# Another written order, with other PSUM slots and masks, for a fused threshold-attention and maxout-FFN kernel

## The chip, the cores and the metric

The kernel runs on one core of a Trainium2 chip. The metric is the device time in microseconds (us) of one execution. The runs of the kernel before took 441.89 to 442.23 us, median 441.96 of three.

The engines are named as in the profile: PE is TensorE (matmuls; PEld are its weight loads), DVE is VectorE, ACT is ScalarE, POOL is GpSimd, and SP issues most of the DMAs. Each engine takes its own instructions strictly in the order in which they are written; between engines semaphores hold an instruction back until its inputs are there and its output buffer is free.

## The reference

Attention over 8 batches, 8 heads, 576 tokens and head size 64, in which only scores within tau = 0.02 of the row's maximum count, and then an FFN whose hidden value is the maximum of three projections:

```python
scores = scale * np.matmul(q, k.transpose(0, 1, 3, 2))
thresh = np.max(scores, axis=-1, keepdims=True) - tau
scores = np.where(scores >= thresh, scores, -1000000000.0)
attn = np.exp(scores - np.max(scores, axis=-1, keepdims=True))
attn = attn / (np.sum(attn, axis=-1, keepdims=True) + 1e-09)
x = np.matmul(attn, v).transpose(0, 2, 1, 3).reshape(4608, 512)
h = np.maximum(np.maximum(x @ w1, x @ w2), x @ w3)      # 512 -> 768
return h @ w_out                                         # 768 -> 512
```

## The kernel before

A batch is handled in two quads of four heads. A quad is nine chunks of 128 rows of two heads each, and a chunk is two halves of 128 rows by 576 scores; in all 144 chunks and 288 halves. The work of the whole kernel is cut into small steps, and one string, `ORDER`, says in which order the steps are written. Every letter is one step; a digit behind a capital letter is the PSUM slot (0 to 3, two banks each) into which a step of TensorE writes. All instructions of an engine are held in this written order, so the string sets five queues at once.

The steps, by letter:

- `l` one load of q, k or v by SP (the tiles `qm`, `km`, `q8`/`k8`, printed as `q_..`/`k_..`, `vm`, `vr`); `g` one load of FFN weights by SP into `stage`; `z` its cast by POOL into `w` or `wo`; `y` a cast of v by POOL (`vb`, `vr`).
- `T` transposes q or k of a quad on TensorE into PSUM (tile `tp`), four such steps a quad. `a` copies q out of the slot on ACT (tile `qt`), `c` copies k out of it, mostly on DVE (tile `kt`); `q` copies `qt` with its partition halves swapped into `qs`, mostly on POOL.
- `S` the scores of one half, on TensorE into a slot (tile `sc`). `m` the row's maximum (or negated minimum), DVE, which also writes the half to SBUF as `z`; a few halves of `z` lie in spare `stage` buffers. Then there are two ways. A half with mask 0 or 2 gets `s` on DVE (a 128x1 threshold, `th`; not for mask 2), `e` on ACT (a steep ramp below the threshold), `n` on ACT (Exp with the row's sum). A masked half, 1 or 3, gets `e` on ACT (Exp) and `k` on DVE (zero below the threshold, and the sum). With masks 2 and 3 `e` reads the PSUM slot itself, so the slot is let go by ACT's `e`; with 0 and 1 by DVE's `m`.
- `r` reciprocal of a chunk's sums, DVE. `p` normalizes one half on POOL (tile `P`, bf16), two a chunk. `t` turns a chunk's P by a transposing DMA of SP into `ptq`.
- `O` the product of P and v on TensorE (tile `o`), four a batch, each reading a quad's nine turned chunks; `w` and `x` copy it out on DVE and ACT (tile `xt`, the FFN's input). All four of a batch must be copied before its first FFN piece.
- `F` the first half of an FFN piece, `B` its second half (the row halves of the array are used by two accumulations, which then change places); 18 hidden pieces (`ph`) a batch, copied out by `h` (ACT) and `v` (DVE, a maximum), and two output pieces (`po`), copied out by `u` (ACT) and stored by `o` (SP). `N`, `j`, `i` are the last ninth of the tokens; `f` and `d` the very last output.

The function `issue` takes a letter, takes the next item of that step's queue, and writes its instructions:

```python
        if what == "S":
            c, r = next(todo["S"])
            c[r] = scores(Ls[c["g"]], c["idx"], r, where)
            line["m"].append((c, r))
        ...
        elif what == "t":
            turned(line["t"].pop(0))
```

`_Ordered` adds the dependence that holds each engine's instructions in this order, so nearly all of them carry its line, L93, in the profile; they are told apart by their tiles. `MASKED` has one digit for each half.

Of the kernel before, what the change touches and what calls it, by code (L numbers as in the profile page):

```python
# [21 lines left out]
FLAT = 2.0 ** -100  # L22

MASKED = """
220202110002002100110000100020020312000112012010100000000010100000001100
001000111010000101100000000000110001100000011110110200100000100010000000
110001101110100100010000001001100100000100101111102300000100100000001000
001000110100100001000000000100100001011110100011011100002100001000001013
"""


# [11 lines left out]
meS0kynS2tssT3snkynkercperlT3pmnpmntqremS0lasprgeT3pmeS2psstnplnS0mzecesqrmS3etqkeS2gpnmS1npsmtnS0prmleS3pmS  # L43
2npsmnS0yrsmetperS2epmO1eqtnkplemnzswT2teS3rplS1empnmS3tpnssrS1klepS0mapermtS2epmT1S3nmqtnkO2qemncpS3txrskT1
peS2rmeS0ptmegpamS2npS1ertsmpnlkzS2elmS3eS0mpnlO1srkepsmnO2tyeprgwnpmT1xS3cpeS0sszmF2eS1meBqkF0ngqT3shrsmBay
S2tvpnF3rpemS1BpemF0pnsvT2BnyctS1esrlsT2mphS3lezS1maF0myntpT2sS3ngrcqF1eBmpnS2svpBnrmS3peS0tmeyF2zmnF3lBsvep
S0rhkBptesF2mgeS1zvF0nsmBpteBsrgvpnF1kS3phS2semBnqmF0S3evqF2ntrmBpelS1spvBnlmS3qhF0rsmepS1tnBpsmS3ezvS2eS1rm
pF0etsyO3mnlkngpO2eswetkBxrmpT3nF2rvpaS1BnqmS0hspS3meF2prS1smntBzesmF3ezvT0tBeclT1yS2pnvS0apsmtS3eyrmlS1epS2
mepF0mnqsmnS3tkBnkeF1restpkumeS2prtBumlperkpS0ustS2umS3pesmS1eqtT0mO2nlpceqsrmO3ntywelkS0pxlS1meF3prnS2smBye
myF0thpskS1oeBpF2nlvF3nlrmBpeBkpS1hstsvS0eF3lrmpnF2mBepBsveF1nT0vBtarkS3lhqS2smleF0prF1mnBysntBveS2plvnS0pom  # L50
F3nyS1pmeBsysmF0thT2rrlpeS1clF3epsmBnqT2svBaS1evqS2nmF0pS3nmqBtnmT2pS1hrcpS3esmS0petF2melS1rmpBnF3skpetF0sve
BlBmnF2vhtF1esrBkpnS0vtT3npBmS2arvpS0ermO3eqtsmepT1swntpS0cF2epesmtnS3kT1nS0mtBessrkpameS3preS1mS0uqmuS3mpnS
1tsmS2pnoS0rempS3lempO1lnkqlemO2lnymeO0srkpetkeF3swxykxpT2BercnprtS1uyS2upmF0termqS3eBymN2lhsskpelkS0eF3ertm
S1pjBlmeS0plvF2npS1mnyF3tpmnBsopT0nvBaS1kF2ieqrssmS0hlpBmelT1qF3snrvF0epcBlepS2vBnpsmtS1nS3rmphS2mnpF1smeS0B
snmF3tevS2T0mF1atBrsekpBevS0thS2pmF3nymS1qeBrsmnpS0tvF2eplF1rmnpBskeBptF3hsvS0eBrsstpmnS1lvT2qeO0mpnlscnT3wS
# [774 lines left out]
```

## Time and profile before

| | |
|---|---|
| median of three runs | 441.96 us |
| profiled execution | 442.03 us |
| its span, first to last instruction | 440.2 us |
| busy: PE / DVE / ACT / POOL | 418.9 / 393.9 / 403.6 / 317.0 us |
| mean granted TensorE clock | 0.988 |
| bytes moved by DMA | 88.50 MB |

How to read it: a line of a group has the operation, the tile written and the tiles read, the shapes and the count, then busy time and the mean ns of one. In a listing by time the first number is the start in us from the span's start, the second the length; rows that follow each other are merged, with their count behind an x. A bracket holds the idle time of the engine just before the row, and what ended it. SPq are instructions of SP's queue: their length is the issue, and the data lands later. PE's matmuls are pipelined and their ends modelled.

### The profile page before, as it was taken

The numbers are of one execution on the slowest core, as the hardware profiler recorded it, in microseconds if no ns is written. First come the engines' busy times: TensorE is split into PE (matmuls) and PEld (weight loads), VectorE is DVE, ScalarE is ACT, GpSimd is POOL, SyncE is SP. The second block draws the span as 40 slices with busy tenths as digits, with TensorE's granted clock in tenths as the row PEclk, the third lists the DMA queues.
The fourth block names the chain that finished last, engine by engine and source line by source line (L and its number), as shares of the span: only waits on it lengthen the run. The fifth ranks groups of instructions, "written<-read, shape, count | busy, mean of one in ns | idle before, by whom it ended". The sixth has DMA issues, their size and how long they took to land.

```text
span 440.2 us, 14283 instructions
## 1 busy us (share of the span) xinstructions
PE 418.9 (95%) x5188; PEld 313.6 (71%) x5190; DVE 393.9 (89%) x1248; ACT 403.6 (92%) x834; POOL 317.0 (72%) x420
## 2 busy tenths in 40 slices
PE   7696789999999999999999999999999999999996
PEld 6353446787788776787678777887688777786873
DVE  4888899999999999999999999999889999998542
ACT  4999999999999999999999999999999998989521
POOL 1988999998787778867786778886585776554400
PEclk9987999999999999999999999999999999999999
DMA  6999999999999999999999999999698778583812
GB/s 190 276 239 214 270 215 260 263 252 252 220 277 224 237 165 242 291 160 232 189 242 238 202 182 273 192 199 208 135 237 153 147 109 185 102 169 72 192 50 85
DMA packets 213959, 88.50 MB, mean 201 GB/s; under 512 B 189184, under 2 KB 202240, under 8 KB 213888
## 3 DMA queue, kind: packets, MB, share of 16 engines
q1 hardware_dynamic: 213360, 86.96, 95.4%
q8 instruction: 41, 0.67, 0.6%
q10 hardware_dynamic: 528, 0.62, 0.5%
q14 instruction: 30, 0.25, 0.2%
HBM read 35.65 MB, written 9.44 MB: 102 GB/s over the span
## 4 chain that ended last, share of the span: by engine, by line
PE 78%; DVE 5%; POOL 5%; issue 4%; ACT 3%; DMA 2%; SPq 1%; DVEq 0%; POOLq 0%; ACTq 0%
PE ph L93 31%; PE sc L93 26%; PE po L93 10%; PE o L93 8%; POOL P L93 4%; PE tp L93 3%; ACT z L93 3%; DVE z L93 3%; DMA qm<-in_q_dram 2%; SPq L93 1%; DVE kt L93 1%; POOL w L93 1%; DVE stage L93 0%; DVE hm L93 0%; POOL qs L93 0%
## 5 line engine op out<-in xcount | busy, mean ns | idle before, releaser
L93 POOL TENSOR_SCALAR P<-z,rs 128x576 bf16<-128x576 f32 x250 | 202.0, 819 | 59.1 <-DVE rs L93 30.4
L93 DVE TENSOR_SCALAR_CACHE_REDUCE z<-sc 128x576 f32<-128x576 f32 x250 | 183.2, 749 | 12.2 <-PE sc L93 8.1
L93 PE MATMUL sc<-kt,qs 64*128 64x256 f32 (+2 forms) x640 | 179.8, 417 | 5.5 <-DVE z L93 3.9
L93 PE MATMUL sc<-kt,qt 64*128 64x320 f32 (+2 forms) x640 | 180.9, 429 | 3.1 <-DVE z L93 1.2
L93 PE MATMUL ph<-xt,w 64*128 64x288 bf16 (+2 forms) x2160 | 172.0, 283 | 0.2 <-DVE hm L93 0.2
L93 PEld LDWEIGHTS <-w 64*128 64x128 bf16 (+1 forms) x2160 | 128.0, 94 | 31.6 <-issue 4.0
L93 ACT ACTIVATE z<-z,th 128x576 f32<-128x576 f32 x161 | 120.5, 767 | 2.2 <-DVE th L93 1.9
L93 ACT ACTIVATE z<-z 128x576 f32<-128x576 f32 x175 | 117.6, 674 | 0.2
L93 PEld LDWEIGHTS sc<-kt,qs 64*128 64x128 f32 (+1 forms) x640 | 92.4, 179 | 22.5 <-DVE z L93 8.6
L93 PEld LDWEIGHTS sc<-kt,qt 64*128 64x128 f32 (+1 forms) x640 | 92.0, 179 | 14.7 <-DVE z L93 3.5
L93 DVE SCALAR_TENSOR_TENSOR z<-z 128x576 f32<-128x576 f32 x75 | 61.7, 827 | 1.4 <-ACT z L93 1.1
L93 POOL COPY qs<-qt 64x640 f32<-64x640 f32 (+3 forms) x66 | 45.9, 695 | 19.5 <-ACT qt L93 16.1
L93 ACT ACTIVATE z<-z,nm 128x576 f32<-128x576 f32 x72 | 53.9, 767 | 0.0
L93 PE MATMUL po<-wo,hT 64*128 64x512 bf16 (+3 forms) x454 | 53.3, 354 | 0.3
L93 DVE TENSOR_TENSOR hm<-ph,hm 128x576 bf16<-128x576 f32 (+2 forms) x54 | 37.0, 685 | 9.8 <-PE ph L93 9.6
L93 ACT ACTIVATE hm<-ph 128x576 bf16<-128x576 f32 (+2 forms) x54 | 31.9, 590 | 14.3 <-PE ph L93 13.8
L93 PEld LDWEIGHTS <-hT 64*128 64x128 bf16 (+2 forms) x456 | 28.4, 95 | 18.5 <-issue 2.6
L93 DVE TENSOR_TENSOR hT<-ph,hm 128x576 bf16<-128x576 f32 (+2 forms) x54 | 36.9, 683 | 2.8 <-PE ph L93 1.0
L93 PE MATMUL o<-ptq,vb 128*64 128x512 bf16 (+2 forms) x544 | 38.7, 282 | 0.2 <-DVE z L93 0.2
L93 POOL TENSOR_SCALAR P<-stage,rs 128x576 bf16<-128x576 f32 x38 | 29.5, 783 | 11.7 <-DVE rs L93 8.4
L93 ACT ACTIVATION_READ_ACCUMULATOR z<-z 128x1 f32 x175 | 33.6, 192 | 0.0
L93 PEld LDWEIGHTS <-vb 128*64 128x64 bf16 x544 | 22.4, 111 | 14.0 <-issue 5.6
(44 smaller groups left out, 412.2 us busy)
## 6 DMA issues: line engine op xcount, KB each, us to landing
vm<-in_v_dram SPq DMA_DIRECT2D x32, 256.0 KB, 4.6
qm<-in_q_dram SPq DMA_DIRECT2D x15, 512.0 KB, 4.7
km<-in_k_dram SPq DMA_DIRECT2D x15, 512.0 KB, 5.4
out_dram<-ob SPq DMA_DIRECT2D x14, 512.0 KB, 4.5
stage<-in_moe_w_dram SPq DMA_DIRECT2D x9, 512.0 KB, 5.6
ptq<-P SPq DMA_TRANSPOSE x144, 4.5
vr<-in_v_dram SPq DMA_DIRECT2D x16, 128.0 KB, 3.8
stage<-in_moe_w_out_dram SPq DMA_DIRECT2D x3, 512.0 KB, 5.5
```

Source lines behind the costliest of these rows:

```text
L93: ins = fn(*a, **kw)
```

## The change

The change gives `ORDER` and `MASKED` other values. The steps, the functions and the tiles stay as they are. The string has the same steps in the same numbers but for three letters: `s` 191 in place of 187, `n` 199 in place of 201, `k` 89 in place of 87. Steps stand a few letters earlier or later than before nearly everywhere, and most slot digits are different. Of the 288 digits of the masks, 0 goes from 187 to 191, 1 stays at 84, 2 goes from 14 to 8 and 3 from 3 to 5: masked halves (1 or 3) are 89 in place of 87, halves whose `e` reads PSUM (2 or 3) are 13 in place of 17.

```diff
 MASKED = """
-220202110002002100110000100020020312000112012010100000000010100000001100
+200201101002000000030000103012000330000120210110100001000000100000010110
...
 ORDER = """
-lllllllllT0laqqlcT1aS2lcqqgmS0S3lemS1lmnT2lmeS3lsaS0mnqlqemT3lyerclcapsnS1lS2eqmlS3qemznmS2perS1mnpsmnpT3ske
-ytS1erkpT2agmnT3pclesqS2aqetS0meqlrnspmS1eqsT2nmpS3tnrcS0zlemS2eprmS3npmtS0npsgS1sermpS2emyS3eptmT0eplmS1ayl
...
+lllllllllT1lcaqqlT0S1alcqqmgS3S0elmlnS1smlT3emS2laS0scnqlmT3qelmyS2anlS0mqelqsmezS1lcnrmS3gperpS1nmS0pesmS2y
+ekT3pknT1tressmparmleqcT2lnS3qkeS1pasmetS2prmelpsS3nlmpnsmS2peT1tssqmelycnS2qezmS1nS0rssptnS2rS3gpemynmetrsp
...
```

How it moves instructions, at three places. The first is DVE's queue at the very start: `qs` and `kt` are the copies of the transposed q and k, and the TENSOR_SCALAR rows are the maxima of the first scores. Before:

```order
L93 MEMSET vr_102 64x64 x2
L93 COPY qs<-qt 64x320
L93 COPY kt<-tp 128x320
L93 COPY qs<-qt 64x256
L93 TENSOR_SCALAR z,nm<-sc 128x576 x4
L93 TENSOR_SCALAR th<-nm 128x1
```

and after:

```order
L93 MEMSET vr_102 64x64 x2
L93 COPY kt<-tp 128x320
L93 COPY qs<-qt 64x320
L93 COPY qs<-qt 64x256
L93 TENSOR_SCALAR z,nm<-sc 128x576 x2
L93 TENSOR_SCALAR th<-nm 128x1
```

The first copy of k now stands ahead of the first copy of q, and the first threshold two maxima earlier.

The second is TensorE's queue where quad 1 is transposed for the first time (in the string `T3`, `T2`, `T3` before and `T3`, `T1`, `T2` after; the order does not print the slots). The rows with `qm` and `q_147` are the transposes of q, those with `km` and `k_149` of k, and `sc` are scores. Before:

```order
L93 MATMUL tp<-identf,qm 128x64 x8
L93 MATMUL tp<-identf,q_147 128x64 x2
L93 MATMUL sc<-kt,qs 128x320
L93 MATMUL sc<-kt,qt 128x256
L93 MATMUL tp<-identf,km 128x64 x8
L93 MATMUL tp<-identf,k_149 128x64 x2
L93 MATMUL tp<-identf,qm 128x64 x8
```

and after:

```order
L93 MATMUL sc<-kt,qs 128x320
L93 MATMUL sc<-kt,qt 128x256
L93 MATMUL sc<-kt,qs 128x256
L93 MATMUL sc<-kt,qt 128x320
L93 MATMUL tp<-identf,qm 128x64 x8
L93 MATMUL tp<-identf,q_147 128x64 x2
L93 MATMUL tp<-identf,km 128x64 x8
L93 MATMUL tp<-identf,k_149 128x64 x2
L93 MATMUL tp<-identf,qm 128x64 x8
```

Two scores that stood among or behind the transposes now stand ahead of them, and the three transposes follow each other, in slots 3, 1 and 2.

The third is SP's queue from the ninth transposing DMA (the last of quad 0) to what follows the eighteenth (the last of quad 1). Before:

```order
L93 DMA_TRANSPOSE ptq<-P 128x9x128
L93 DMA stage<-in_moe_w_dram 128x4x256
L93 DMA_TRANSPOSE ptq<-P 128x9x128
L93 DMA km<-in_k_dram 128x2x512
L93 DMA_TRANSPOSE ptq<-P 128x9x128 x2
L93 DMA vm<-in_v_dram 64x4x256
L93 DMA_TRANSPOSE ptq<-P 128x9x128
L93 DMA vm<-in_v_dram 64x4x256
L93 DMA_TRANSPOSE ptq<-P 128x9x128
L93 DMA q_902<-in_q_dram 128x4x64
L93 DMA_TRANSPOSE ptq<-P 128x9x128 x4
L93 DMA stage<-in_moe_w_dram 128x4x256
```

and after:

```order
L93 DMA_TRANSPOSE ptq<-P 128x9x128
L93 DMA km<-in_k_dram 128x2x512
L93 DMA_TRANSPOSE ptq<-P 128x9x128 x5
L93 DMA vm<-in_v_dram 64x4x256
L93 DMA_TRANSPOSE ptq<-P 128x9x128 x4
L93 DMA stage<-in_moe_w_dram 128x4x256
L93 DMA vm<-in_v_dram 64x4x256
L93 DMA q_1040<-in_q_dram 128x4x64
L93 DMA k_1042<-in_k_dram 128x4x64
L93 DMA qm<-in_q_dram 128x2x512
```

Between the ninth and the eighteenth there stand two other DMAs in place of five; one `stage` load has moved ahead of the ninth, and a `vm`, the `q` and others now follow the eighteenth.

More of the change, by code (lines that the diff above doesn't have):

```diff
@@ L24 @@
 MASKED = """
[L25 to L28 removed]
+200201101002000000030000103012000330000120210110100001000000100000010110
+001001100010001010110000000000110000110010111010001000100000100010000100
+100000111101000100010000001001010000000101101101111000101000010000001000
+001001111011000010000000001000100000010101210010010011002000010100101031
 """
@@ L46 @@
[L46 to L55, printed above, removed]
@@ new lines @@
+ptS0resmS2pesmepS3tmepS1rmnpT0tknO3qersmteqkapS2wntS1pslerS3mpnmS2ptnsmS1perT0smS3eptmnpcO1eztrsekS0qemS2xmp
+ntS1mpegS0rmnplS3nmplemlS0qnrsS1klpT2egmO3elpsmaS0knqO2rwetpmeS1pxsrskS3epF2emS0ynmT1pBnmzS3hrcF0eymT2qBgask
+F3peS1sveBtprsmS2ezvnT1F0mpnT3BctapS2hrkqS3ntF0meslrpmT2eS1gzcBnsmS3eptS2vnpF1gmnS0psrsmeS3pseBmqF2esmS0tpeB
+vyF3nmS1hrkBpnF2tveF0pmBntyBsvnqS3lrF1eyrsmpS2hsBptemF0lpesS3vBnzlsmF2nlvS1pnS3rmqBetmF0phgS1npBmeS3yvS2etS1
+srmepF0lknpO3mezsnmO2terkpBgwxF1epvT3S2ktaBrnmlqS0hssS3rpmeF2spS1tsemByemzF3nvT0tBpecS1pnvT2tS0qamlS3ezmS1es
@@ new lines @@
+mS2tnF0knkteS3rmBlpesrpmnF1qmuepsskS3etpBuslrmnqS0suopS2umlS3eprmS1eT0pmtO2npcoemO3lnwerkS1pxtS0smeF2lpemS3F
+1nsrmpBkS0yhF3mntyBseBrlvF2peS0vpnS1mpF3nsBsmyeT0ykBhF1alsvF2elrrBkpeBkF3htvS0nBlpmeF1lprvS2eBpmnF3tpsveS0ys
+nS2mS1emqBnF0mqhtT2rsS1epcBnpmtF3npT2rsvlBaS1srlevqS2emF0pS3nmptBempT2S1hscpS3nmF2yteqmS0nBmF3tesrS1svpleF0s
+mpnBBketyF2vhF1erBktpnS0vBepmT3S2asvtS0emT3eO1rcptnkpleF3mnrwpS0nskS2peT1trBsmaeqmS0erpsS1umtpS2umpeS0meS3qm
+S1ntqS2mnoS0pmeS3lrsmO1nplseplmO2eysmxkO0etkelsrwF1xpekpT3nkS0tnrBmeycynqS2kF0ulpuS3smlBnprmS1epN2smteprshkS
@@ L74 @@
+nO1kyxeO3ewtperspS0xtpS2nmF3pnmS1tBesmF2oekS0hS1srsmpnBtS3yevopF0emN2eknrmF1ptjBpeS3F2nmBvBhtF3skeF1rveBpiBs
+nvpO2hkS0erwpS1rnmF2tpnmS3peBmF1pnsrS0vpteBmF3pnsS2vteBmS0hsS1rmpteF2mF3pnBsnsS1erF0vpBetmpBnvF2hS1keBmS3tnF
+0srvpeF1mBepBvyO3hskO0ertS1xwpnS2mpnF3mS0eF1rspmeBpBtevS2nS0vS3kF1tmsF2meknBmerpekBupukN3rrO0jpuO1pxuO3wptF1
+opF2hF0xvF1vtF2hF0vF3vF2hF0vF3vtF1hF2ovF0vF1hF3vF0vF2hF3vO1vO0wF2xF0uF3hF2voF0vF3hF2ivF0vF1hF2vF0vF1hF2vF0vF
+1hF2vF3vF0hF2vF3vF2uF1ouN2ofjdi
 """
```

37 lines of the change are left out of this document (16 added, 21 removed).

## The prediction

> **What bounds the kernel now.** I read the page first, then the windows, then the waits of TensorE, then the first 72 us instruction by instruction.
>
> ```profile
> PE 418.9 (95%) x5188; PEld 313.6 (71%) x5190; DVE 393.9 (89%) x1248; ACT 403.6 (92%) x834; POOL 317.0 (72%) x420
> ```
>
> Four engines are busy for most of the span, so the shares alone decide nothing. The windows split it (columns: length, then PE, PEld, DVE, ACT, POOL busy with counts, TensorE's granted clock, DMA share, GB/s):
>
> ```profile
> 24.00:64.00 40.00, 31.18 (x265) 17.42 (x263) 36.02 (x123) 39.59 (x84) 37.70 (x49) 0.91 1.15 235
> 72.00:100.00 28.00, 27.43 (x370) 21.99 (x368) 26.49 (x87) 27.67 (x60) 26.12 (x36) 1.00 1.20 260
> 100.00:121.00 21.00, 21.00 (x260) 16.47 (x257) 19.98 (x67) 20.78 (x43) 17.53 (x24) 1.00 1.14 234
> 121.00:248.00 127.00, 126.73 (x1694) 98.44 (x1690) 123.77 (x390) 125.19 (x257) 97.95 (x130) 1.00 1.10 225
> 248.00:316.00 68.00, 67.93 (x892) 52.06 (x890) 66.58 (x213) 66.98 (x137) 51.83 (x67) 1.00 1.02 199
> 316.00:371.00 55.00, 55.00 (x718) 41.87 (x714) 50.94 (x161) 53.32 (x112) 40.31 (x55) 1.00 0.83 163
> 411.00:436.00 25.00, 24.90 (x218) 18.22 (x218) 11.96 (x26) 7.44 (x17) 1.34 (x2) 1.00 0.37 103
> ```
>
> The head, up to 64, is not TensorE's: it stands idle for 8.8 of 40 us while ACT has no gap (39.59). From 72 on TensorE is full. Its waits say the same: in the window 88 to 420 this is the only line, in the whole run the longest line is the second (total us, times, longest).
>
> ```profile
> PE ph L93 <- DVE hm L93: 0.2, 1, 0.2
> ...
> PE sc L93 <- DVE z L93: 5.1, 9, 1.2
> ```
>
> So the time is a head, in which FFN pieces don't exist yet, and then TensorE's fixed work. The matmuls are the same in number and shape after the change; what can move is when the first FFN piece starts, and whether TensorE stays full afterwards.
>
> ```profile
> 67.14 1.18 PE L93 MATMUL o<-ptq,vb 128*64 128x512 bf16 x16
> 71.32 0.65 PE L93 MATMUL ph<-xt,w 64*128 64x288 bf16 x8
> 119.44 2.73 PE o L93 x21
> ```
>
> These are the third product of batch 0 (67.14), the first FFN piece, and the products that close batch 1.
>
> **The change, part by part.** *The first scores.* The rows of the start:
>
> ```profile
> 5.42 0.44 ACT L93 ACTIVATE qt<-tp 128x320 f32<-128x320 f32 x1 [1.34 <-PE tp L93]
> 5.89 0.32 DVE L93 COPY qs<-qt 64x320 f32<-64x320 f32 x1 [4.22 <-ACT qt L93]
> 6.20 0.22 PE L93 MATMUL tp<-identf,km 64*128 64x64 f32 x1
> 6.24 0.49 DVE L93 COPY kt<-tp 128x320 f32<-128x320 f32 x1
> 6.79 0.48 PE L93 MATMUL sc<-kt,qs 64*128 64x256 f32 x1 [0.36 <-DVE kt L93]
> ```
>
> Now DVE copies `kt` after `qs`, which waits for ACT. After the change `kt` comes first: it can start at 5.42 with the ACT row, ends at 5.91, `qs` ends at 6.23, and TensorE's second transposes end at 6.42. The first score goes at about 6.45 in place of 6.79: -0.3 us, and ACT's first Exp with it.
>
> *The slot of the third transposes.* The rows around 20 to 24 us:
>
> ```profile
> 20.11 0.47 PE L93 MATMUL tp<-identf,qm 64*128 64x64 f32 x8 [1.16 <-ACT qt L93]
> 20.66 0.81 DVE L93 COPY kt<-tp 128x640 f32<-128x640 f32 x1
> 21.53 0.79 PE L93 MATMUL sc<-kt,qs 64*128 64x256 f32 x1 [0.96 <-DVE th L93]
> 23.10 0.76 DVE L93 TENSOR_SCALAR_CACHE_REDUCE z<-sc 128x576 f32<-128x576 f32 x1 [1.56 <-PE sc L93]
> 24.11 0.74 POOL L93 TENSOR_SCALAR P<-z,rs 128x576 bf16<-128x576 f32 x1 [1.24 <-DVE th L93]
> 24.15 0.78 ACT L93 ACTIVATE z<-z,th 128x576 f32<-128x576 f32 x1 [0.33 <-DVE th L93]
> ```
>
> The third transposes of quad 1 (`T3`) go to slot 3, which the first ones (`T3`, a few letters before) still hold until ACT's `qt` copy; the next score (`S2`) goes to slot 2, held by `T2` until DVE's `kt` copy. TensorE stands twice, DVE loses 1.56, POOL 1.24, ACT 0.33. After the change the three are written `T3`, `T1`, `T2`: slot 2 was last a score's, so the third finds it free, and the following scores use slots 3 and 1, let go earlier. I take these waits as gone: ACT -0.3, POOL -1.2. Bounds: nothing saved if another slot is late there, and at most DVE's 1.5.
>
> *The DMA queue.* All transposing DMAs and loads of SP are issued in one row, and the queue is late. The eighteenth transposing DMA, last of batch 0's four products' inputs, closes the row at 59.07; the third product starts 67.14.
>
> ```profile
> 44.94 0.53 SPq L93 DMA_DIRECT2D stage<-in_moe_w_dram  x1
> 47.89 0.54 SPq L93 DMA_DIRECT2D km<-in_k_dram  x1
> 53.27 0.64 SPq L93 DMA_DIRECT2D vm<-in_v_dram  x1
> 56.29 0.62 SPq L93 DMA_DIRECT2D vm<-in_v_dram  x1
> 58.39 0.59 SPq L93 DMA_DIRECT2D q<-in_q_dram  x1
> 59.07 5.81 SPq L93 DMA_TRANSPOSE ptq<-P  x4
> ...
> DMA to landing us min/median/max: 3.2/4.5/8.2
> ```
>
> The row ends at 64.88; with 3.2 to landing from the issue of its last quarter (about 63.5) it lands at 66.7, just before 67.14: this queue sets the third product. Between the ninth and the eighteenth transposing DMA five other issues stand now, two after the change (`km`, one `vm`): -0.53-0.64-0.59 = -1.8 us. Ahead of the ninth one `stage` load more stands: +0.5. The fifth waits for its P, which POOL gives 1.2 earlier. Net -1.8+0.5-1.2 = -2.5 at the eighteenth, or -1.3 if POOL's gain is lost. The postponed loads stand between the eighteenth and the thirty-sixth: 20 issues in place of 18, +1.2 there, so that the thirty-sixth is -1.3 earlier at best and as late as now at worst (its row is shown below).
>
> *ACT before the first FFN piece.* That piece needs the second `xt` copy of ACT. Two neighbouring passes show the step:
>
> ```profile
> 61.88 0.76 ACT L93 ACTIVATE z<-z,th 128x576 f32<-128x576 f32 x1
> 62.55 0.77 ACT L93 ACTIVATE z<-z,nm 128x576 f32<-128x576 f32 x1
> ```
>
> One pass is 0.67. Counted in the written order, 85 passes (49 `e`, 36 `n`) stand ahead of that copy now and 82 (48, 34) after: -3 x 0.67 = -2.0. With 0.3 from the start and 0.3 from the slot: -2.6 on ACT. SP gives -2.5, so nothing holds the first FFN piece back by more than a tenth: I take -2.3, 71.32 to about 69.0. Ends: -1.3 (SP without POOL's gain) and -3.2 (DVE's 1.5 in place of ACT's 0.3, plus one score less on TensorE).
>
> *From there to the products at 119.44-122.* Ahead of the last of them 147 passes stand now, 145 after; so between 71 and 121 ACT has 62 in place of 61, +0.7, in windows where it is full (27.67 of 28, 20.78 of 21). Gain left: -1.6. DVE has two max passes and one `kt` copy more there (37 and 4 now, 39 and 5 after): 2 x 0.76 + 0.81 = 2.3 by the rows at 23.10 and 20.66, against 2.5 us that it stands idle in 72 to 121 (26.49 of 28, 19.98 of 21). I cost it at nothing, but its cover is nearly used up. What the rest needs of the masked pass and of P, and the end of the DMA queue's late stretch:
>
> ```profile
> L93 DVE SCALAR_TENSOR_TENSOR z<-z 128x576 f32<-128x576 f32 x75 | 61.7, 827 | 1.4 <-ACT z L93 1.1
> ...
> L93 POOL TENSOR_SCALAR P<-z,rs x250: 734/744/1891, 13.0 to 411.6; 128x576 bf16<-128x576 f32 x125
> ...
> 109.95 4.43 SPq L93 DMA_TRANSPOSE ptq<-P  x3
> ```
>
> *The rest.* Masked halves go from 87 to 89 in all: 2 x 0.67 less on ACT, 2 x 0.83 more on DVE; four `th` more. From 121 to 371 ACT has 4.5 us idle and DVE 8.7, TensorE 0.3, so this lies beside TensorE: 0. The slots rewritten within five letters of being let go are 66 before and 67 after: no reason for more waits or fewer. The last 25 us are FFN pieces with one max each, TensorE 24.90 of 25, in the same counts: 0.
>
> **Sum.** -2.3 + 0.7 = -1.6. The profiled execution took 442.03 (span 440.2 and 1.8 around it), 0.07 above the median 441.96: 442.03 - 1.6 - 0.07 = 440.4 us.
>
> **The rivals.**
> *Given back at once.* Between the first FFN piece and 121 us DVE, ACT, SP and TensorE are all near full. If DVE keeps the 2.5 us idle that it has there and has 2.3 more to do, the whole -2.3 goes: 442.0. For it: the idle shares. Against: DVE's waits there are mostly for scores that TensorE writes when ACT and DVE have freed a slot, so they shrink when DVE is late; and the queue is no limit, since its last row of three ends at 114.4, and with 3.2 to 4.5 from its last issue it lands by 117.5, 2 us ahead of 119.44.
> *New waits for PSUM slots in the full part (slower).* Every slot choice is new, and now only 0.2 us of waits stand there, a best case. A wait costs 5.1 / 9 = 0.57 (the line above). Three of them cancel the gain, from five on the kernel is slower by over 0.2%; six give 440.4 + 3.4 = 443.8. Against: the equal counts of tight slots.
> *DVE and POOL in each other's way.* P takes 744 ns at the median and 1891 at most. The longest stand beside DVE's masked pass, which reads `z` twice. The head has one masked half more ahead of the first FFN piece (13, not 12); if it falls on a P of the late stretch, POOL loses 1891-744 = 1.1 us, of which half reaches the queue: 440.9. [...]
>
> **How the numbers follow.** About 0.2% (0.9 us) is what a measurement of this kernel can tell from no change. Chances: forecast 0.48 (438.8 to 441.1), given back 0.24, new slot waits 0.22, DVE and POOL 0.06. Faster by over 0.2%: 0.45 of the first, 0.03 of the second, 0.04 of the last, 0.52. Same: 0.03 + 0.19 + 0.02 = 0.24. Slower: 0.02 + 0.22 = 0.24. The range begins at 442.0-3.2 = 438.8 and goes to 443.0, which leaves out the part of the third case with more than five waits.
>
> **What would show it.** Right: the first FFN piece near 69.0; no wait of TensorE for `qt` near 20 us; the eighteenth transposing DMA issued near 61; TensorE's window 121 to 371 still without waits. Wrong: a first FFN piece at 71 or later (the head's steps fail), or TensorE lines in the waits of 88 to 420 that add up to over 1.6 us (the rival with the slots).

## The result, and the profile after

The changed kernel takes 444.99 us (median of four runs, 444.17 to 445.08) where the kernel before took 441.92 on the same chip: 1.0065 times, 95% interval 1.0047 to 1.0082. It is 3 us slower; the forecast was 1.6 faster. The profiled execution took 444.99, its span is 443.2 us.

The page's first line, and the windows that were shown of before:

```profile
PE 423.1 (95%) x5190; PEld 321.7 (73%) x5190; DVE 397.9 (90%) x1256; ACT 402.9 (91%) x830; POOL 312.6 (71%) x420
...
24.00:64.00 40.00, 31.89 (x252) 19.73 (x252) 35.35 (x120) 39.24 (x84) 38.65 (x50) 0.83 1.04 230
72.00:100.00 28.00, 27.64 (x376) 21.55 (x376) 27.15 (x88) 28.00 (x61) 26.59 (x35) 1.00 1.13 231
121.00:248.00 127.00, 126.56 (x1680) 99.51 (x1678) 123.04 (x391) 124.66 (x258) 95.57 (x129) 1.00 1.15 223
316.00:371.00 55.00, 54.09 (x698) 43.16 (x696) 53.01 (x164) 53.55 (x113) 38.90 (x55) 1.00 0.76 156
```

TensorE is still full from 72 on, but in 316 to 371 it now stands 0.9 us, where it stood for nothing. In the head its granted clock is 0.83, not 0.91. The waits of TensorE, first of the window 88 to 420, then of the whole run (total us, times, longest):

```profile
PE tp L93 <- DVE th L93: 0.9, 1, 0.9
PE o L93 <- DMA ptq<-P: 0.4, 1, 0.4
```

```profile
PE sc L93 <- DVE z L93: 5.9, 8, 1.3
PE tp L93 <- DVE z L93: 4.4, 3, 3.0
...
PE warm L93 <- DVE kt L93: 0.6, 1, 0.6
```

Two new lines in the full part make 1.3 us, fewer than the 3.0 that were lost. The waits listed are a part of the loss only, so a better measure is the start of the same piece of TensorE in both traces (pieces counted by kind; products four a batch). This table is worked out from the starts in each kernel's trace; the other columns are experiments that follow:

| start in before, us | piece | after | before_cold | warm_in_slot_0 | queue_order_old | three_repairs | from_152_unmasked | before_kt_first_warm8 |
|---|---|---|---|---|---|---|---|---|
| 6.79 | first score | +0.51 | +0.48 | -0.19 | -0.14 | -0.10 | +0.06 | -0.01 |
| 67.14 | third product | -0.89 | +1.95 | -1.98 | -1.84 | -2.24 | +0.07 | -0.64 |
| 71.32 | first FFN piece | -0.54 | +1.95 | -1.64 | -1.50 | -1.89 | +0.07 | -0.64 |
| 120.75 | eighth product | +0.28 | +1.95 | +0.17 | +0.83 | -1.13 | +0.03 | -1.06 |
| 166.11 | twelfth product | +1.24 | +1.95 | +1.59 | +0.83 | -1.13 | +1.03 | -1.06 |
| 266.11 | twentieth | +1.77 | +2.32 | +2.06 | +1.29 | -0.44 | +1.56 | -1.01 |
| 316.65 | twenty-fourth | +1.54 | +2.34 | +1.82 | +1.06 | -0.67 | +1.32 | -0.99 |
| 368.31 | twenty-eighth | +3.00 | +2.37 | +3.28 | +2.52 | -0.34 | +1.66 | -0.97 |
| 440.2 | end of the span | +3.0 | +2.4 | +3.3 | +2.5 | -0.3 | +1.6 | -0.9 |

For after it reads: 0.5 ahead at the first FFN piece (2.3 were forecast), that lead gone by 121, then 1.0 lost up to 166, 0.3 to 316, and 1.5 between 316 and 368. Four places of this trace follow; the stretch from 72 to 121 comes with the experiments.

**The start.** By time, after:

```profile
1.05 4.02 PE L93 MATMUL warm<-vr 128*128 128x128 bf16 x36 [1.05 <-DVE vr L93]
...
5.96 0.49 DVE L93 COPY kt<-tp 128x320 f32<-128x320 f32 x1 [4.29 <-PE tp L93]
...
6.50 0.37 PE L93 MATMUL warm<-vr 128*128 128x128 bf16 x2 [0.58 <-DVE kt L93]
6.81 0.37 PE L93 MATMUL tp<-identf,qm 64*128 64x64 f32 x1
...
7.29 0.74 PE L93 MATMUL sc<-kt,qs 64*128 64x256 f32 x1
```

The first score's matmul lasts 0.74 us, in before 0.48: TensorE is at half clock until about 10.5 us (its transposes take 0.22 us from 11 us on, and 0.31 to 0.37 ahead of that; 0.31 is what they take at 35.8, where the granted clock is 0.50), while in before the warming matmuls got shorter, 0.22 and not 0.31 us, at about 4. And the two warming matmuls that follow the first transposes wait for DVE's `kt` copy. They are written to slot 3; `T1` puts its k transposes there, while before's `T0` used 0 and 2.

**A stop in the head, and half clock behind it.** The third transposes of quad 1, DVE's work ahead of them, and the clock behind them (columns: length, PE busy, granted clock, DMA share, GB/s):

```profile
18.52 1.42 DVE L93 SCALAR_TENSOR_TENSOR z<-z 128x576 f32<-128x576 f32 x1
...
21.49 0.73 DVE L93 TENSOR_SCALAR_CACHE_REDUCE z<-sc 128x576 f32<-128x576 f32 x1
```

```profile
22.28 0.47 PE L93 MATMUL tp<-identf,qm 64*128 64x64 f32 x8 [3.02 <-DVE z L93]
```

```profile
24.00:25.00 1.00, 1.00 (x6) 0.57 1.32 310
25.00:26.00 1.00, 1.00 (x5) 0.50 1.05 395
26.00:27.00 1.00, 0.93 (x4) 0.50 1.06 361
27.00:28.00 1.00, 0.82 (x10) 0.72 1.93 143
```

The slot held a score, as the prediction said, and that score's maximum (21.49) stands late on DVE: TensorE waits 3.0 us in place of 1.2 and 1.0. From 24.1, some 2 us behind that stop, the clock is half for 2 x (0.43 + 0.50 + 0.50 + 0.28) = 3.4 us. That stretch isn't new: before has one as long behind its two shorter waits, from 21.1 on.

```profile
21.00:22.00 1.00, 0.47 (x2) 0.54 1.07 366
22.00:23.00 1.00, 1.00 (x6) 0.50 1.33 284
23.00:24.00 1.00, 1.00 (x6) 0.50 1.29 213
24.00:25.00 1.00, 1.00 (x14) 0.75 0.73 113
```

Between 10.5 and 48 us, before has two stretches at half clock (from 21.1 and from 38.2) and after has three that begin there (from 24.1, 34.4 and 44.6). What is new here is the longer stop. No run put this slot back, so its price was not measured.

**The eighteenth and the fifty-fourth transposing DMA.**

```profile
57.21 5.80 SPq L93 DMA_TRANSPOSE ptq<-P  x4
```

```profile
161.29 2.74 SPq L93 DMA_TRANSPOSE ptq<-P  x2
```

```profile
165.38 0.38 PE L93 MATMUL o<-ptq,vb 128*64 128x512 bf16 x1
166.15 0.69 PE L93 MATMUL o<-ptq,vb 128*64 128x512 bf16 x7 [0.38 <-DMA ptq<-P]
```

The row with the eighteenth closes 1.9 us earlier than in before (63.01, not 64.88). The row that ends with the fifty-fourth closes at 164.03, where in before it was issued alone and closed at 161.68:

```profile
160.41 1.27 SPq L93 DMA_TRANSPOSE ptq<-P  x1
```

In after the third product of batch 2, the eleventh of all and the first to read these nine, starts one matmul and stops. The lateness is the queue's: in after the P of the fifty-fourth was done at 160.82 and its DMA was issued at 162.69; in before P was done at 160.39 and the DMA was issued at 160.41.

**The masked pass at 351.6.**

```profile
351.15 2.18 POOL L93 TENSOR_SCALAR P<-z,rs 128x576 bf16<-128x576 f32 x3
...
351.56 2.38 DVE L93 SCALAR_TENSOR_TENSOR stage<-stage 128x576 f32<-128x576 f32 x1
...
353.86 0.68 DVE L93 COPY kt<-tp 128x512 f32<-128x512 f32 x1
...
354.60 0.46 PE L93 MATMUL tp<-identf,qm 64*128 64x64 f32 x8 [0.91 <-DVE th L93]
```

A masked pass takes 0.83 us at the mean in before; this one takes 2.38, and POOL's three P beside it take 0.73 each, as alone (median 0.74). Before's trace already has a long one, of 1.43 us at 168.6, beside a P of 0.74 (168.67). In after three are longer than 1.4: this one, one of 1.56 at 370.2, and the one of 1.42 shown above. DVE's next instruction, the `kt` copy, lets slot 0 go, and the next transposes want slot 0.

### The profile page after: what moved, and what is told of

Same layout as the page of the kernel before. It is cut to its first block, busy times and chain, and to the rows that moved or that the text cites. A ratio compares the mean times of both kernels' runs of the same rounds, so it can differ in the third digit from the quotient of the medians.

```text
span 443.2 us, 14308 instructions
## 1 busy us (share of the span) xinstructions
PE 423.1 (95%) x5190; PEld 321.7 (73%) x5190; DVE 397.9 (90%) x1256; ACT 402.9 (91%) x830; POOL 312.6 (71%) x420
## 4 chain that ended last, share of the span: by engine, by line
PE 65%; POOL 11%; ACT 8%; issue 5%; DVE 5%; DMA 4%; SPq 1%; POOLq 0%; DVEq 0%; ACTq 0%
PE ph L93 24%; PE sc L93 21%; PE po L93 9%; POOL P L93 8%; PE o L93 7%; ACT z L93 5%; DMA ptq<-P 4%; DVE z L93 3%; PE tp L93 3%; POOL qs L93 2%; PE warm L93 1%; ACT stage L93 1%; POOL w L93 1%; DVE stage L93 1%; SPq L93 1%
## 5 line engine op out<-in xcount | busy, mean ns | idle before, releaser
L93 POOL TENSOR_SCALAR P<-z,rs 128x576 bf16<-128x576 f32 x250 | 199.5, 810 | 67.1 <-DVE rs L93 29.8
L93 PE MATMUL sc<-kt,qt 64*128 64x320 f32 (+2 forms) x640 | 183.9, 432 | 3.5 <-DVE z L93 2.7
L93 PE MATMUL sc<-kt,qs 64*128 64x256 f32 (+2 forms) x640 | 183.1, 422 | 4.2 <-DVE z L93 3.2
L93 ACT ACTIVATE z<-z,th 128x576 f32<-128x576 f32 x170 | 127.7, 768 | 3.7 <-DVE th L93 3.0
L93 ACT ACTIVATE z<-z 128x576 f32<-128x576 f32 x177 | 119.2, 675 | 0.3
L93 PEld LDWEIGHTS sc<-kt,qs 64*128 64x128 f32 (+1 forms) x640 | 93.4, 181 | 20.3 <-DVE z L93 7.5
L93 PEld LDWEIGHTS sc<-kt,qt 64*128 64x128 f32 (+1 forms) x640 | 93.6, 181 | 17.3 <-DVE z L93 8.8
L93 ACT ACTIVATE z<-z,nm 128x576 f32<-128x576 f32 x68 | 51.6, 767 | 0.0
L93 PE MATMUL o<-ptq,vb 128*64 128x512 bf16 (+2 forms) x544 | 39.7, 281 | 1.0 <-DVE z L93 0.6
L93 PEld LDWEIGHTS <-vb 128*64 128x64 bf16 x544 | 24.9, 111 | 12.8 <-issue 5.8
```

The lines of the kernel that those rows point to most:

```text
L93: ins = fn(*a, **kw)
```

## The experiments

Theories: R, the new order loses behind 88 us, at places that can be named; H, the new head loses, by a late start that is paid at the end. For hybrids the string was cut at places where both have written nearly the same steps; the steps between were put at the cut, and each half keeps the mask that it had when its maximum was written.

### Old head, new rest; new head, old rest; new from 152 us

The three cuts, each with the letters ahead of it, what stood behind it, and what stands there now (in the first the digits 2 and 3 are exchanged behind the cut, so that no slot is in use twice):

```diff
 mF2eS1meBqkF0ngqT3shrsmBay
-S2tvpnF3rpemS1BpemF0pnsvT2
+F2pS1veBprsmS3ezvnT1F0mpnT2Bctap
...
 ynmT1pBnmzS3hrcF0eymT2qBga
-skF3peS1sveBtprsmS2ezvnT1F0mpn
+tseksS2tvpnF3rpemS1BpemF0pnsvT2
...
 petF0sveBlBmnF2vhtF1esrBk
-pnS0vtT3npBmS2arvpS0ermO3eqtsmepT1
+tpnS0vBepmT3S2asvtS0emT3eO1rcptnk
```

> The written order, slots and masks of before up to the letter ahead of its second FFN-related stretch (about 69 us: 462 letters), those of after from there on. Theory R (the rest loses: TensorE's idle behind 88 us grows from 9.7 to 12.0 us, in TensorE's own order of after, the head is worth 0.1): 442.0 + 2.4 = 444.4, between 443.8 and 445.2. Theory H (the head loses: its cold and slow TensorE clock, and a thinner lead of ACT and DVE over TensorE, which is only paid later): 442.0, not above 442.5.

> The mirror: the order of after for the head (460 letters), that of before from there on. Theory R: 441.4 to 442.2, as before. Theory H: 444.5 to 445.2, as after.

> The order of before for 1022 letters (to about 152 us), that of after from there on. Theory R by TensorE's idle of after less before, window by window: 0.3 of the loss lies between 88 and 153, 2.1 behind, so 442.0 + 2.1 = 444.1. Theory H: 442.0.

Measured, as ratios to the kernel before in the same session: 1.0082 (1.0050 to 1.0113), 1.0020 (1.0005 to 1.0036) and 1.0052 (1.0039 to 1.0064), which are +3.6, +0.9 and +2.3 us. R holds in its main point: the new rest costs 2.3 us without anything of the new head. The first is 1.2 above its forecast; close behind the cut, at 74.5 us, the transposes of q wait 0.87 us for a `qm` load. The second fits neither theory (R 441.4 to 442.2, H 444.5 to 445.2). Its profile, which is its longest run (445.00), led by 1.54 at the first FFN piece and was 2.14 late at the fifth product, behind the cut. So a cut has a price of its own: the first tells only the sign of the new rest, and the second tells nothing on the new head.

The third was foretold to 0.2 us, but in part by luck. The forecast counted what TensorE stands in this window in after, the wait for the fifty-fourth transposing DMA with it. In the hybrid that DMA is issued in time (160.52) and the eleventh product doesn't wait; instead a score at 159.21 waits 0.72 us for a maximum of DVE that stands behind two masked passes (0.87 and 1.22 us). It loses 1.0 us up to the twelfth product there, and 1.2 more between the twenty-fourth and the twenty-eighth, where the masked pass stands.

### The masked pass

```diff
-...F3nkT0pBecS1hsrp...
+...F3nT0pBeckS1hsrp...
```

> After, with one DVE pass moved: the masked pass that took 2.38 us at 351.6 (beside three P of POOL) is written behind the kt copy and not ahead of it. Theory L (DVE stood in that pass for POOL's three P, and the kt copy behind it kept the next transposes' slot): the masked pass may still be long, but the kt copy ends near 352.9 and not 354.5, TensorE's 0.9 wait for that slot goes, and the time falls by 0.7 to 1.2 us: 443.9. Rival (the wait is TensorE's order alone, and moves to the next score): within 0.2 of after, 445.0.

Measured 1.0046 (1.0023 to 1.0070), against 1.0065 of after; the intervals overlap. By the trace the first half of theory L is right:

```profile
351.50 2.18 POOL L93 TENSOR_SCALAR P<-z,rs 128x576 bf16<-128x576 f32 x3
...
352.56 0.69 DVE L93 COPY kt<-tp 128x512 f32<-128x512 f32 x1 [0.58 <-PE tp L93]
...
353.17 1.12 DVE L93 SCALAR_TENSOR_TENSOR stage<-stage 128x576 f32<-128x576 f32 x1
...
353.77 0.44 PE L93 MATMUL tp<-identf,qm 64*128 64x64 f32 x7
```

The copy ends at 353.25, the transposes don't wait, and the masked pass, which now meets only the end of POOL's three, takes 1.12. But a score at 355.43 now waits 0.57 us for POOL's `P`. Between the twenty-fourth and the twenty-eighth product the kernel loses 1.07 us, where after loses 1.46: of 0.7 to 1.2 expected, 0.4 was won. The half was then made plain, in two kernels (one digit of the masks, one `s`, an `n` for the `k`):

```diff
-001001111011000010000000001000100000010101210010010011002000010100101031
+001001111011000010000000001000000000010101210010010011002000010100101031
...
-ptmBnpmF3S0etsqvBespmF1ntS2pvS0ermBpnS3mqF2hktF0peS1meBmBnvO1nstrsesprvF2eywpF3nkT0pBecS1hsrp...
+ptmBnpmF3S0etsqvBespmF1ntS2pvS0ermBpnS3mqF2hktF0peS1meBmsBnvO1nstrsesprvF2eywpF3nnT0pBecS1hsrp...
```

> The kernel with the order of before up to 152 us and of after from there (2.4 us over before in its own runs), with the half of 351.6 us made plain. Theory L alone, in a kernel whose queue is on time: the wait for th at 352 us goes, 0.8 to 1.2 less: 1.4 us over before. Rival: the gap is taken up by the next wait, 2.4 over before.

Measured 1.0023 (0.9993 to 1.0054): +1.0 us, against +2.3 of the same kernel with the masked pass. In the table, between the twenty-fourth and the twenty-eighth product, it loses 0.34; the same kernel with the masked pass loses 1.23, and after, `warm_in_slot_0` and `queue_order_old`, which have it too, lose 1.46 each. Theory L: 0.9 to 1.1 us, from one instruction. The time intervals of the two kernels overlap, so it is the trace that tells.

### The queue of SP

```diff
-...S1svpleF0s
+...S1svpeF0s
...
-...ktpnkpleF3mnrwp... S1ntqS2mnoS0pme...
+...ktpnkpeF3mnrwp...  S1ntqllS2mnoS0pme...
```

> After, with two small loads of the next batch (the 57th and 58th l) written behind the 54th transposing DMA, not ahead of it. In after that DMA is issued 2.3 us later than in before and lands at 166.0, while the last product of batch 2 wants to start at 165.7; that product's wait and what follows it made 0.7 us in one profile of after and 1.5 us in two of its hybrids. Theory Q (the queue of SP, not PSUM slots, makes this loss): the DMA is issued some 1.3 us earlier, the wait for ptq at that product goes, and the time falls by 0.7 to 1.5 us against after, to about 443.8. Rival (the gap only moves to the next DVE wait, as in the hybrid that was cut at 152 us, where 0.9 us stood two pieces earlier): within 0.3 us of after.

Measured 1.0094 (1.0064 to 1.0123), above after's 1.0065, though the intervals overlap. The row of which the fifty-fourth is the last:

```profile
151.01 15.73 SPq L93 DMA_TRANSPOSE ptq<-P  x9
```

Nine transposing DMAs stand in a row without a gap and end at 166.7. The queue was late long before the two loads, so moving them freed nothing; the product still waits 0.49 us (at 168.87). This profile's run was one of the longest of its kernel (448.99; the others 444.4 to 450.8), 0.45 us later at the first FFN piece than before. So it shows the backlog and not what the two loads cost. With the plain half as well:

> The same, and the half whose masked pass took 2.38 us at 351.6 is made plain (one digit of the masks; its pass goes from DVE to ACT, with one th more). This takes the wait for POOL away and not only its order. Theories Q and L together: 0.7 to 1.5 and 0.9 to 1.2 less than after: 442.4, between 441.9 and 443.2. If only one holds, 443.5 to 444. If neither: 445.

Measured 1.0032 (1.0011 to 1.0054), +1.4 us: the unmasking holds again (0.33 lost between the twenty-fourth and the twenty-eighth product), and the product still stands for 1.05 us (at 166.79). The third try takes the order of all loads and stores between the thirty-seventh and the fifty-fourth from before:

As it stands in SP's queue (`t` a transposing DMA, `l` a load, `o` a store, numbered):

```diff
-t37 l46 o1 l47 t38 o2 l48 t39 l49 t40 l50 l51 l52 t41 l53 l54 t42 t43 t44 l55 l56 t45 t46 t47 l57 t48 ... t51 l58 t52
+t37 t38 l46 t39 l47 l48 t40 o1 l49 l50 t41 l51 t42 l52 l53 t43 l54 o2 t44 l55 l56 t45 t46 l57 t47 l58 t48 ... t52
```

> After, with the loads and stores of SP put back between the 37th and the 54th transposing DMA as before has them (12 loads and 2 stores of the same stretch; every DMA of that kind stays where it was). In after the queue is 1.9 us late at the 36th and 5.8 us late at the 43rd, with the same number of issues between: only which of them stand ahead differs, two stores and three loads sooner. Moving only the last two loads did not free the 54th, since the queue was late through all of 116 to 166. Theory Q: the 54th is issued by 161.2 (162.7 in after), the product that waits 1.0 to 1.5 us for it waits under 0.4, and the time falls by 0.8 to 1.5: 443.9. Rival (it stays late, since POOL gives its P later too and DVE sets that): the 54th at 162 or later, no change.

```profile
161.85 1.36 SPq L93 DMA_TRANSPOSE ptq<-P  x1
...
165.70 1.16 PE L93 MATMUL o<-ptq,vb 128*64 128x512 bf16 x16
```

The fifty-fourth is issued 0.65 later than foretold, but in time: the product runs through. Between the eighth and the twelfth product this kernel loses nothing (+0.83 at both), after loses 0.96 and `warm_in_slot_0`, with the new queue order, 1.42. In time it is 1.0058 (1.0037 to 1.0079), no more than 0.3 below after, since this profile has lost 2.3 us already between the first FFN piece and the eighth product:

```profile
102.76 1.96 POOL L93 TENSOR_SCALAR P<-z,rs 128x576 bf16<-128x576 f32 x2 [1.72 <-DMA ptq<-P]
...
102.92 1.19 DVE L93 SCALAR_TENSOR_TENSOR z<-z 128x576 f32<-128x576 f32 x1
```

Again a masked pass beside two P, and each gets slower (1.19 us, and 0.98 for a P); behind them TensorE stands 0.59 us at an FFN piece at 107.19. This is one place of the 2.3 us; the others were not followed.

### The start

```diff
-                warmed(2)
+                warmed(2, 0)
```

> After, with the two warming matmuls that follow the first transposes written to PSUM slot 0. They use slot 3, which in after holds the first k transposes (T1 takes slots 1 and 3) until DVE's kt copy, so that they and the second transposes behind them wait; in before T0 takes slots 0 and 2 and nothing waits. Theory W (this wait is why the first score came at 7.3 and why TensorE's clock went up only at 10 us in four of six profiles with this head, in none of three with the old one): second transposes near 5.9, first score at 6.4 to 6.6 with the clock up by 6.6, first FFN piece near 69.6; of the time at most 0.5 less, since the lead is given back by 121 us: 444.3 to 444.8. Rival (the clock's switch is chance alone): first score 6.6 or 7.3 as it falls, no change.

```profile
5.58 0.29 PE L93 MATMUL warm<-vr 128*128 128x128 bf16 x2
...
5.97 0.24 PE L93 MATMUL tp<-identf,qm 64*128 64x64 f32 x1
...
6.59 0.48 PE L93 MATMUL sc<-kt,qs 64*128 64x256 f32 x1 [0.16 <-DVE qs L93]
...
69.68 0.66 PE L93 MATMUL ph<-xt,w 64*128 64x288 bf16 x8
```

The wait is gone, and the numbers came as theory W said: 5.97, 6.59, 69.68. In time 1.0047 (1.0018 to 1.0076), +2.1 us; the interval overlaps after's, and the profile (+3.3 at the end of its span) is no shorter than after's (+3.0), so no gain in time is shown. The clock: among seven profiles with the new head and slot 3 four came up at 9.6 to 10.5 us and three at 3.7 to 5.4; with slot 0 all of four at 4.5 to 5.5; with the old head and 36 warming matmuls all of eight by 6.2. So the wait may make late starts likelier, and it doesn't make them certain; these are few profiles. In the four late ones the clock was still low at the first transposes (5.0 to 5.7 us), ahead of the wait, so the wait can only have held it back from there on.

The wait by itself costs little. Where it stands and the clock is up at 3.8 to 4.1 us (`queue_order_old`, `headnew_restold`), the first score comes at 6.65, against 6.59 and 6.68 without it (`warm_in_slot_0`, `three_repairs`). After's +0.5 there goes with the late clock.

What a late start costs, in before:

```diff
-WARM = 36
+WARM = 6
```

> Before, with 6 warming matmuls ahead of the first transposes in place of 36, so that TensorE's clock is still half when the first scores are due, as it was until 10.0 us in the profile of after. It prices that cold start. Theory C (the cold start is paid in full, since the head is a chain): the first score near 7.3, the first FFN piece about 1 us later than 71.3, and the end 0.7 to 1.2 later, 442.9. Rival (the head's delay is taken up by TensorE's idle before 88 us): 442.0 within 0.3.

Measured 1.0041 (1.0028 to 1.0055), +1.8 us. Its transposes take 0.31 us up to 11.5 us, and 0.24 from 11.7 on. The first FFN piece is 1.95 late, not 1, and the table's column shows 1.95 at every piece up to 166 and 2.3 to 2.4 from there on: this order passes that delay on nearly unchanged.

### All three repairs

The queue's order, the plain half and slot 0 together:

> After with the queue's order put back, the half of 351.6 us made plain and the warming in slot 0. If theories Q, L and W name the whole loss: 442.0 to 443.0. If the rest of the loss is spread over many small waits: 443.3 to 444.2.

Measured 1.0021 (1.0006 to 1.0036): 442.86 us beside 442.10. Of after's 0.65% two thirds are gone, and the intervals of the two don't overlap. The profile is the fastest of its ten runs (441.64); it is 0.3 us shorter than before's (span 439.9), and the only line of TensorE's waits in 88 to 420 is

```profile
PE o L93 <- issue: 0.2, 1, 0.2
```

It still loses 0.7 us between the twelfth and the twentieth product. The nineteenth starts at 263.85, and the last turned P of its quad lands at 264.38; in before the product started at 264.83, 1.6 behind a landing at 263.25. That transfer took 5.2 us from its issue here and 3.6 there. This place was not tried.

### Where the lead goes

Three kernels with the order of after ahead of a cut and that of before behind it (the last two with the warming in slot 0, the second with the queue's old order too):

```diff
 S2umlS3eprmS1eT0pmtO2npcoem
-O3lnwerkS1pxtS0smeF2lpemS3F1nsrm
+yerO3ntywekS0pxlS1mseF3prnS2mBy
...
 vpeF0smpnBBkeltyF2vhF1erB
-ktpnS0vBepmT3S2asvtS0emT3eO1rcptn
+kpnS0vtT3npBmS2arvpS0ermO3seqts
...
 vS1pnS3rmqBetmF0phgS1npBme
-S3yvS2etS1srmepF0lknpO3mezsnm
+S3ezvS2seS1rmpF0etsyO3mnlnkgpO2e
```

> The order of after up to the products that close batch 1 (804 letters, 121 us), that of before from there. With the warm start the head of after had its first FFN piece at 69.8 and the eighth product 0.3 us ahead of before. Theory G (the head's gain is given back by 121 us): 441.5 to 442.0, no difference from before. If the head's gain were kept: 440.5.

> After with the queue's order put back and the warming in slot 0, up to 152 us (1024 letters); the order of before from there on. In the profile of the three repairs the eighth product came at 119.6, 1.1 us ahead of before, and nothing was lost up to 180. Theory K (a lead that is kept to 152 us is worth its length at the end, since TensorE is full from there): 441.0 to 441.8 where before has 442.1 to 442.5. Rival (the lead is eaten in most executions, or at the seam, as it was in the hybrid cut at 121 us): 442.3 to 443.2.

> The order of after up to 97 us (636 letters) with the warming in slot 0, that of before from there on. Theory K: the lead at 97 us (about 1.4) is kept at least in part, 441.2 to 442.0. Rival (between 97 and 121 us DVE and POOL collide and eat it, 0.9 us at one FFN piece in two profiles with this head): 442.4, no difference from before.

Measured 1.0040 (1.0025 to 1.0056), 1.0032 (1.0009 to 1.0056), 1.0029 (1.0008 to 1.0050): all slower than before by 1.3 to 1.8 us. The first had a late clock (first score at 7.50, 0.74 us long) and lost 1.4 us between the eighth and the twelfth product, behind its cut. `repaired_to_152` led by 1.96 at the first FFN piece and by nothing at the eighth product; `repaired_to_97` led by 1.23 and was 1.2 behind at the fifth product, close behind its cut, and 2.5 at the eighth. The lead of the new head is eaten between 72 and 121, in part or whole, in every profile that has it (`three_repairs` kept most, 1.1 of 1.9). So theory K was not put to the test by these, since no lead was left at the cuts.

The step of the start alone, in before:

```diff
-lllllllllT0laqqlcT1aS2...
+lllllllllT0lcaqqlT1aS2...
```

> Before, with the first step of the change alone: DVE copies the first kt ahead of the first qs (one letter moved; the transposes keep slots 0 and 2). By the prediction's first step the first score goes at 6.45 to 6.65 in place of 6.79. Theory S (an earlier start is worth its length in the head and little at the end, since the lead is eaten by 121 us): first FFN piece 0.1 to 0.3 earlier, the time within 0.3 us of before. Rival (the head's chain carries it through, as the late start of the cold clock was carried through with 1.9): 0.2 to 0.3 less.

> The same with 8 warming matmuls behind the first transposes in place of 2. TensorE has nothing else to do there until the second q and k land at 5.9, and 8 take 0.45 us at the full and 0.86 at the half clock. If cold starts are what spreads the times of before (from 441.3 to 446.5), fewer of them: median as before or 0.3 less, and the upper runs gone. If not: no difference, or 0.1 to 0.3 more where the warming delays the second transposes.

Measured 0.9985 (0.9967 to 1.0004) and 0.9979 (0.9957 to 1.0002): 441.98 and 441.83 beside 442.31, and the intervals just hold 1. The profile of the second, in the table's last column, led by 0.64 at the first FFN piece

```profile
70.67 0.65 PE L93 MATMUL ph<-xt,w 64*128 64x288 bf16 x8
```

and by 1.06 to 0.97 from 99 us to the end: in the old order a lead that is there at 121 is kept to within 0.1 us in this column, and the delay of `before_cold` to within 0.4. Between 72 and 121 a shift of the old order does change: -0.06 becomes +0.27 in the profile of `before_kt_first`, and -0.04 becomes +0.64 in that of `before_warm8`. The first score was not earlier in either (6.77 and 6.78; 6.45 to 6.65 were expected). It needs both copies, and the order of the two does not bring the later one forward unless the first begins earlier: `kt` began at 5.87 and 5.88, since the transposes ended near 5.8 at a lower clock (in `before_kt_first_warm8` the first two take 0.32 and 0.33 us, in before 0.24 and 0.27), `qs` ended at 6.7. Two more parted the edits:

> Before with 8 warming matmuls behind the first transposes and its own order (kt behind qs). It parts the two edits of the last pair. If the warming does it: 0.4 us less than before, as with both (441.83 beside 442.31). If kt first does it: as before.

> Kt first and 12 warming matmuls, 0.7 us of them at the full clock, 1.3 at the half clock. If a busier TensorE ahead of the first scores brings the clock's switch forward, as good as 8 or better: 0.3 to 0.6 less than before. If 12 delay the second transposes (due at 5.9), 0.1 to 0.4 worse than with 8.

Measured 1.0004 (0.9994 to 1.0014) and 0.9993 (0.9984 to 1.0003). Warming alone gives nothing. The three kernels with `kt` first are all a little below before, none beyond doubt. No version was shown to beat the kernel before.

## Why the prediction was wrong, step by step

*The first scores* (-0.3). The order of the copies was read rightly, but the score needs both, and two things were left out that stand beside them: the warming matmuls behind the first transposes, which use slot 3, now taken, and TensorE's clock, which came up 6 us later in the profile. Measured +0.5 at the first score and +1.4 at the fifth. Where the clock is up by 4.1 us with the wait, or by 5.5 without it, it is -0.10 to -0.19; in `kt_before_masked`, with the wait and transposes of 0.31 us up to 5.4, it is +0.12. So the late clock is most of it. The prediction quoted no row of the warming, though the change altered a slot digit in that very place: T0 to T1.

*The slot of the third transposes* (ACT -0.3, POOL -1.2). Wrong: "slot 2 was last a score's, so the third finds it free". A score's slot is free when its maximum is done, and that stood on DVE behind two masked passes (one of 1.42 us), two thresholds, two reciprocals and another maximum. TensorE waits 3.02 in place of 2.1. POOL, which was to save 1.2, waits 1.54 near there (at 20.87; 1.24 in before). What the step cost at the end is open.

*The DMA queue* (-2.5 at the eighteenth). Right: its row closes 1.9 us earlier (63.01), with the five other issues down to two. The third product came 0.9 earlier (with a good start 2.0) and no longer waited for it: the eighteenth lands at 64.95, 1.3 ahead of the product, where in before it landed at 66.83 and the product started at 67.14. The sentence on the rest of the queue was wrong, though: it followed the queue to the thirty-sixth, found it at most as late as now, and set no price for what lies behind. Between the thirty-seventh and the fifty-fourth the two stores and eight of the loads stand ahead of an earlier transposing DMA than in before, and the new order there cost 1.0 (0.96 between the eighth and the twelfth product, 0.00 with the old order put back).

*ACT before the first FFN piece* (-2.3 in all). The passes were counted rightly, 82 for 85. ACT starts its first transposed q at 5.89, not 5.42, and its second 1.1 later. Measured -0.5 at the first FFN piece; in four profiles whose start was good -1.2 to -2.0. The mechanism was right, its size too large by 0.3 to 1.1, and the profile of after fell short of these by the start.

*From there to 121* (gain left 1.6). The rival "given back at once" was the better one: from -0.5 to +0.3 in after, from -1.6 to +0.2 and from -1.5 to +0.8 in two kernels whose start was good. Its reason, DVE's cover of 2.5 us against 2.3 more to do, was named and called nearly used up, and the cost still set to nothing. `queue_order_old` shows one place of it, a masked pass that meets two P (0.59 of 2.3 us), and no run changed that place. `three_repairs` kept 1.1 of 1.9 with the same steps there. So what eats the lead stays open.

*The rest* (0). This is the step that made the sign. It was argued from idle shares over 250 us (ACT 4.5, DVE 8.7) and from equal counts of tight slots, 66 and 67. Neither says anything on one late instruction: 1.0 us came from a queue that was 5.8 us late at the forty-third transposing DMA (issued at 139.20, in before at 133.41), and 0.9 to 1.1 from one masked pass that took 2.38 us beside POOL's three P. Of the 2.7 us that after loses behind 121 some 0.6 was not traced to a place. The rival "new waits for PSUM slots" gave the nearest time of the rivals (443.8, 1.2 short) with the wrong cause: the slot at 354.6 was late since DVE's masked pass took 2.38 us. The rival "DVE and POOL in each other's way" had the cause, with the price on the wrong engine: POOL was to lose 1.1, half of it hidden; it was DVE that lost 1.6, and DVE stands between two steps of TensorE. The price itself was too high for one pass: before's P of 1891 ns, the third of a row of 3.38 us from 320.60 on, stands beside two masked passes, one behind the other (from 322.01 and 322.69, 0.75 each). The prediction's own sign of this (waits in 88 to 420 over 1.6 us) did not show, with 1.3: here the wait rows held less than TensorE lost.

At 351.6 POOL's row had begun 0.4 us earlier and kept its 0.73 a pass, and DVE's masked pass took 2.38. It lasted through nearly all of POOL's row: begun at 351.56, ended at 353.94, 0.6 us behind the end of the third P (353.33).

## What to carry to other kernels

Where TensorE is full and its idle is below a microsecond, a new order is worth what its worst few single instructions cost, and shares of idle time over long windows say nothing on that. For each place where the order changes, follow the instruction that lets a slot go or lands an operand: what stands ahead of it in its queue, back to where that queue was last empty, and which engine's work beside it can lengthen it without a semaphore, as at 351.6, where DVE's masked pass took 2.38 us beside POOL's three P, and in `kt_before_masked` 1.12 beside the end of them. An order that has been tuned to one fixed timing also has to be judged by how it takes a shift: in the old one a lead or a delay that was there at 121 us passed through the 300 us behind it within about 0.4, in the new one most leads of the head were eaten within 50.

## What was not expected of the hardware

TensorE's clock in the head. In after the stretches at half clock behind the start have one of two lengths: 3.4 us from 24.1 on (the four rows above) and from 34.4 on, and twice that here, from 44.6 on:

```profile
44.00:48.00 4.00, 2.67 (x14) 1.52 (x16) 3.93 (x14) 4.00 (x10) 4.00 (x5) 0.58 1.16 250
48.00:52.00 4.00, 4.00 (x27) 3.21 (x24) 3.46 (x15) 3.69 (x9) 4.00 (x6) 0.57 1.20 324
```

In the second row TensorE is busy for all of 4.0 us and bounds the head. It does so in before too, at half clock, from 38 to 42:

```profile
38.00:39.00 1.00, 1.00 (x8) 0.58 1.29 279
39.00:40.00 1.00, 1.00 (x14) 0.50 1.31 257
40.00:41.00 1.00, 1.00 (x10) 0.50 0.82 159
41.00:42.00 1.00, 1.00 (x4) 0.50 0.53 78
```

TensorE was at work ahead of the half clock. Ahead of the one at 24.1 it was busy for 1.66 us of four,

```profile
20.00:24.00 4.00, 1.66 (x18) 1.02 (x19) 4.00 (x15) 3.97 (x8) 2.93 (x4) 1.00 1.07 223
```

and for 1.8 of the 3.41 us just ahead of it. The changes of the clock in before and in after, up to 80 us, stand 3.41 us or a multiple of it apart, so both traces can be cut into stretches of 3.41 us from the first change on. The clock was halved behind five of these stretches, in which TensorE was busy for 1.57 and 0.70 us (before, from 17.67 and 34.74) and for 1.80, 1.06 and 1.69 us (after, from 20.73, 30.97 and 41.21). In the others at full clock it was busy for 1.94 us or more, and the clock stayed. At the start, with the same 36 warming matmuls, the clock was up at about 4 us in before and not by 5.1, where they end, in after.

The granted clock of the profile's rows does not show the late start: it is 1.00 in

```profile
6.00:8.00 2.00, 1.50 (x14) 1.03 (x13) 1.12 (x3) 0.79 (x3) 0.47 (x2) 1.00 0.95 251
```

of after, where transposes take 0.31 and not 0.22 us. It has to be read from the lengths of the matmuls.

Times of these kernels also spread differently from run to run: before 441.3 to 446.5 over all sessions with most within 1 us, `kt_before_masked` 442.9 to 446.7, `loads_behind_t54` 444.4 to 450.8. What of this is the clock's start, what the DMAs, was not settled.
